# A fused attention, FFN and expert kernel on one Trainium2 core: output clearing, row crossings and GpSimd subtractions put at other places

## The chip, the core and the metric

The kernel runs on one core of one Trainium2 chip. The metric is the device time of one execution in microseconds (us). The engines are named as in the profile: PE (TensorE), ACT (ScalarE), DVE (VectorE), POOL (GpSimd) and SP (SyncE, which here only issues transfers).

## The reference

Three stages follow each other; all data are float32.

```python
# attention: q, k, v are 2 x 8 x 768 x 64; keys seen: the 96 before a row, and the first 8
scores = scale * np.matmul(q, k.transpose(0, 1, 3, 2)) + bias   # ALiBi slopes per head
scores = np.where(is_global | is_local, scores, -1e9)
x = softmax(scores) @ v                     # then 1536 tokens x 512
# gated FFN, d_ff 1536
xn = x / rms * rms_g
x = (silu(xn @ w_gate) * (xn @ w_val)) @ w_out
# router: top 2 of 8 experts, with noise; w1 is 8 x 512 x 1024, w2 is 8 x 1024 x 512
for e in range(E):
    for k in range(2):
        mask = top2[:, k] == e
        h = np.maximum(x[mask] @ w1[e], 0.0)
        out[mask] += top2_w[mask, k, None] * (h @ w2[e])
```

## The kernel before

**Stages.** Attention goes by tiles of 128 rows (L300 to L610): SP loads `kn`, `qn`, `vn` of a tile (L309, L310, L317), PE turns them (L379), makes scores (L427), turns the probabilities (L454) and multiplies with the values (L491). Between these matmuls PE does FFN work of tokens that are ready (`pz` L698). The FFN's weights come in as `rg`, `rv`, `ro` (SP, L630, 512 KB each) and are converted by `conv` (ACT L635, then DVE and POOL); the last of them come while the FFN runs on its own, in the stretch from 200 to 340 us. A routing stage (L793 on) then puts each token's row number and weight into a table in DRAM.

**Two halves of a number.** A product is made of three: each float32 operand is split into an upper part (a copy on ACT) and the rest (a subtraction), and PE multiplies upper with upper, lower with upper and upper with lower. For expert weights `split` (L672) makes `sa` (of w1) and `sb` (of w2): ACT copies (L677), and DVE or POOL subtracts (L681). Which engine subtracts is in one line:

```python
pool = u == 0 and f < 5 if key[0] == "b" else u > 2 and f < 3
```

**Units.** The experts' work goes by `Unit`s n = 0 to 8, each over eight slices f = 0 to 7 of the 1024 hidden columns. Units 2 to 8 have at most 480, 448, 424, 408, 392, 384 and 368 tokens. For each f, `up` multiplies the tokens with a slice of w1 (`pz`, L1034; ACT makes `zh` L1041, DVE `zl` L1042) and `down` multiplies with w2 (`ac`, L1074). The f of unit n run while the tokens of unit n+1 are made ready in `side(f)` of the main loop (L1254 on):

- `gather` (L977): POOL fetches the rows of the tokens from DRAM into `xg`, one indirect transfer per tile of 128 tokens; for units 3 on the rows lie as 16-bit halves.
- `cross` (L982): SP turns a tile by a transposing transfer, `hg<-xg` (L987).
- `turn` (L989): ACT puts the halves together (`xc`, L755) and copies the upper part (`gh`, L996); DVE subtracts (`gl`, L997). `gh` and `gl` are what `up` of unit n+1 reads first.
- `moe2_weights` (L925): SP loads w1's and w2's slice f of unit n+1 (`wab`, L927 and L932, 256 KB each).

**Results.** A unit's result is copied to `oT` as 16-bit halves (ACT L1133, DVE L1131, filled up by a POOL memset L1118), turned by SP transfers `ob<-oT` (L1144) and put together by ACT (`pb`, L1137) at f = 2 and 3 of the next unit; POOL has fetched the tokens' earlier sum (`y<-out_dram`, L1011), DVE adds (L1103), and POOL writes the rows back (`out_dram<-y`, L1107). Rows are added to what is there, so `out` is set to zero once: `clear_out` (L268), one 3 MB transfer on SP's queue, called at L1213.

**What sets the order.** Each engine does its instructions in program order, and a scheduler has put them in that order when the kernel was built; transfers of one issuing engine go out in the order of its program. `follow(a, b)` (L224) makes a stand behind b in the order; it costs no wait by itself. `marks` is the list of the ACT copies of the FFN's hidden blocks (L711), in the order in which they are written down.

Of the kernel before, what the change touches and what calls it, by code (L numbers as in the profile page):

```python
# [10 lines left out]
F32 = mybir.dt.float32  # L11
# [10 lines left out]
P = 128  # L22
# [85 lines left out]
def fused(ctx: ExitStack, tc: tile.TileContext, q, k, v, n_global, n_local, w_gate, w_val, w_out,  # L108
          rms_g, w_router, w_noise, noise, w1, w2, out):
    nc = tc.nc  # L110
# [111 lines left out]
    state = {}  # L222

    def follow(a, b):  # L224
        tc.add_manual_dep(a, b.name, mybir.DependencyInfo(mybir.DependencyClass.NoSync, mybir.DependencyReason.DATA),
                          reason="order")

    def seq(inst):

        if state.get("strict"):  # L230
            if "seq" in state:
                follow(inst.ins, state["seq"])
            state["seq"] = inst.ins
        return inst
# [31 lines left out]
        nc.sync.dma_start(metad.rearrange("(p n) t -> p n t", p=P), dum)  # L266

    def clear_out():  # L268
        nc.sync.dma_start(out.rearrange("(p t) (c d) -> p (t c) d", p=P, d=P),
                            zero.rearrange("p (o d) -> p o d", o=1).broadcast_to([P, NT // P * DC, P]))  # L270

    chosen = keep.tile([P, NT // P, 2, E], F32, name="chosen")
    flag = keep.tile([P, 1], F32, name="flag")
# [398 lines left out]
    def split(key, u):  # L672
        pid = "ab" + key[1:]
        src = raw[pid][:, "ab".index(key[0])]
        f = int(key.split("_")[1])
        wp = pools["b"].tile([P, 2, 512], F32R, name=f"s{key}_{u}", tag="ws", bufs=3)
        cp = nc.scalar.activation(wp[:, 0], src, AF.Copy)  # L677
        if u == 0 and f < 2:
            follow(cp.ins, marks[-4])
        pool = u == 0 and f < 5 if key[0] == "b" else u > 2 and f < 3  # L680
        (nc.gpsimd if pool else nc.vector).tensor_sub(wp[:, 1], src, wp[:, 0].bitcast(F32))  # L681
        return wp[:, 0], wp[:, 1]

    x2t = {}
# [2 lines left out]
    halved = []  # L687
# [248 lines left out]
    class Unit:  # L936
# [45 lines left out]
        def cross(self, s):  # L982
            m = -(-self.tiles[s][1] // 16) * 16
            if s % 2 == 0:
                self.hw = sb.tile([P, 2, 2 * DC, P], U16, name=f"hg{self.n}_{s}", tag="words", bufs=2)
            self.words[s] = self.hw[:, s % 2]
            nc.sync.dma_start_transpose(self.words[s][:, :, :m], self.xg[s][:m])  # L987

        def turn(self, s, behind=None):  # L989
            m = self.tiles[s][1]  # L990
            xg = self.xg.pop(s)
            ss = slice(s * P, s * P + m)
            if self.halved:
                x3 = sb.tile([P, DC, P], F32, name=f"xc{self.n}_{s}", tag="wc", bufs=2)
                merge(x3, self.words[s], m, behind)
                nc.scalar.activation(self.gh[:, :, ss], x3[:, :, :m], AF.Copy)  # L996
                nc.vector.tensor_sub(self.gl[:, :, ss], x3[:, :, :m], self.gh[:, :, ss].bitcast(F32))  # L997
                return
            pt = ps.tile([P, 512], F32, name=f"pg{self.n}_{s}", tag="to"[s % 2])
            p3 = pt.rearrange("p (a b) -> p a b", a=DC)[:, :, :m]  # L1000
            for c in range(DC):
                mm = nc.tensor.transpose(p3[:, c, :], xg[:m, c * P:(c + 1) * P], ident[:m, :m])
                if behind is not None:
                    follow(mm.ins, behind)
            nc.scalar.activation(self.gh[:, :, ss], p3, AF.Copy)
            nc.vector.tensor_sub(self.gl[:, :, ss], p3, self.gh[:, :, ss].bitcast(F32))
# [248 lines left out]
    for i, u in enumerate(units):  # L1255
# [3 lines left out]
        def side(f):  # L1259
            if nxt is not None:  # L1260
                if i == 1:
                    if f == 0:
                        nxt.slots()
                        for s in range(len(nxt.tiles)):
                            nxt.gather(s)
                        for ti in range(G0[LEAD + 1], NT // P):
                            halve(ti, nxt.last.ins)
                elif i and f == (3 if i == 2 else 0):
                    nxt.slots(behind=halved[-1][0] if i == 2 else None)
                    for s in range(len(nxt.tiles)):  # L1270
                        nxt.gather(s)
                if i and f == 6 and i + 2 < len(units):
                    name(units[i + 2])
                    units[i + 2].fetch()
                if i == 1:
                    for s in range(len(nxt.tiles)):
                        if f == 6 + s // 2:
                            nxt.turn(s, u.mark)
                elif i == 0:
                    if f == FB2 - 1:  # L1280
                        for s in range(len(nxt.tiles)):
                            nxt.turn(s, u.mark)
                else:
                    if f in (3, 4):
                        for s in range(len(nxt.tiles))[2 * f - 6:2 * f - 4]:
                            nxt.cross(s)
                    if 8 - len(nxt.tiles) <= f:
                        nxt.turn(f - 8 + len(nxt.tiles), u.act)
            if nw is not None and (i > 1 or f >= AHEAD):
                moe2_weights(nw.wkey, nw.e, f, halved[-1][1] if i == 2 and f == 0 else None)  # L1290
        u.run(side)
    fast.close()

# [86 lines left out]
```

## Time and profile before

| what | value |
|---|---|
| three runs | 769.32, 774.5, 777.71 us; median 774.5 us |
| the profiled execution | 774.73 us |
| its span in the profile | 773.0 us (1.73 us of the execution lie outside) |
| PE busy | 738.5 us, 96% of the span |
| DVE, ACT, POOL busy | 492.3, 408.5, 322.9 us |
| mean granted PE clock | 0.984 of full speed |
| DMA | 107.98 MB, mean 140 GB/s |

A timeline row has the start in us, the duration in us, the engine, the line, the operation with out<-in, and the count of instructions drawn together; in brackets stands how long the engine had been idle before and what ended that. "SPq" is SP's queue of issued transfers: its duration is the time that issuing took, not the time of the transfer. Line numbers are those of the kernel before. The profile comes from one execution, so sums made from it are compared with its own 774.73 us.

### The profile page before, as it was taken

How to read it: one execution, taken by the hardware profiler on the slowest of the kernel's cores; microseconds unless marked ns; L12 is line 12 of the kernel's file. 1: busy time of each engine (PE TensorE's matmuls, PEld its weight loads, DVE VectorE, ACT ScalarE, POOL GpSimd, SP SyncE). 2: the span in 40 equal slices, each digit the busy share in tenths (PEclk: the TensorE clock that was granted, in tenths of full speed). 3: DMA queues.
4: the chain of work that ended last, by engine and by line, in shares of the span. 5: the costliest groups of instructions: out<-in, count | busy, mean ns of one | idle time of the engine just before them, and what ended most of it. 6: DMA issues, size and time to landing. Idle time of an engine off the chain costs nothing.

```text
span 773.0 us, 13551 instructions
## 1 busy us (share of the span) xinstructions
PE 738.5 (96%) x4763; PEld 668.9 (87%) x4763; DVE 492.3 (64%) x1128; ACT 408.5 (53%) x878; POOL 322.9 (42%) x356
## 2 busy tenths in 40 slices
PE   9889989999999999999999999996999999989993
PEld 6679889999988888889999889885999999989993
DVE  7778887887587887334444667733555556666642
ACT  6667657776453443114331465534575767766640
POOL 3237752341476565011633144442254546353511
PEclk9989999999999999999999999998999999999998
DMA  8955365643343330011235413899686979797211
GB/s 195 286 148 141 99 152 93 128 90 73 113 123 106 113 106 0 1 39 71 56 55 116 158 29 104 282 324 204 170 209 165 293 192 328 194 306 171 78 40 37
DMA packets 183160, 107.98 MB, mean 140 GB/s; under 512 B 114193, under 2 KB 165393, under 8 KB 183088
## 3 DMA queue, kind: packets, MB, share of 16 engines
q1 hardware_dynamic: 174240, 84.61, 43.5%
q0 software_dynamic: 7120, 19.32, 8.3%
q10 hardware_dynamic: 1728, 3.15, 1.3%
q8 instruction: 39, 0.64, 0.4%
q14 instruction: 33, 0.27, 0.1%
HBM read 75.23 MB, written 16.49 MB: 119 GB/s over the span
## 4 chain that ended last, share of the span: by engine, by line
PE 78%; DVE 5%; issue 5%; DMA 4%; ACT 3%; SPq 2%; POOL 1%; POOLq 0%; ACTq 0%; DVEq 0%
PE pz L698 16%; PE pz L1034 15%; PE acc L725 12%; PE ac L1074 10%; PE pg L698 5%; PE pv L698 5%; PE ac L1051 4%; PE ps L427 3%; DMA hg<-xg 2%; PE po L495 2%; PE lg L809 1%; PE pt L379 1%; SPq L932 1%; PE po L491 1%; ACT p L434 1%
## 5 line engine op out<-in xcount | busy, mean ns | idle before, releaser
L1034 PE MATMUL pz<-gh,sa 128*128 128x256 f32 (+7 forms) x576 | 153.4, 335 | 0.0
L1034 PEld LDWEIGHTS pz<-gh,sa 128*128 128x128 f32 x576 | 103.8, 188 | 4.6
L1034 PE MATMUL pz<-gl,sa 128*128 128x256 f32 (+7 forms) x288 | 96.3, 336 | 2.0 <-DVE gl L997 2.0
L1074 PE MATMUL ac<-zh,sb 128*128 128x480 f32 (+4 forms) x320 | 86.5, 363 | 6.1 <-ACT sb L677 6.1
L725 PE MATMUL acc<-wo,dh 128*128 128x512 f32 x288 | 88.1, 398 | 0.5 <-ACT dh L711 0.5
L698 PE MATMUL pz<-xTh,wg 128*128 128x256 f32 x352 | 75.6, 291 | 0.5 <-DVE u L708 0.5
L698 PE MATMUL pz<-xTh,wv 128*128 128x256 f32 x352 | 74.7, 290 | 0.0
L1041 ACT ACTIVATE zh<-pz 128x256 fp32r<-128x256 f32 (+7 forms) x72 | 35.1, 487 | 73.9 <-PE pz L1034 73.9
L1042 DVE SCALAR_TENSOR_TENSOR zl<-pz,zh 128x256 fp32r<-128x256 f32 (+7 forms) x72 | 39.7, 551 | 51.6 <-ACT zh L1041 51.3
L681 DVE TENSOR_TENSOR sb<-wab,sb 128x512 fp32r<-128x512 f32 x67 | 48.8, 729 | 32.7 <-ACT sb L677 30.9
L1074 PEld LDWEIGHTS ac<-zh,sb 128*128 128x128 f32 x320 | 60.6, 191 | 9.9 <-ACT sb L677 6.6
L698 PEld LDWEIGHTS pz<-xTh,wg 128*128 128x128 f32 x352 | 60.2, 196 | 2.8 <-DVE u L708 0.8
L1107 POOL DMA_INDIRECT out_dram<-y,me x30 | 33.8, 1128 | 64.5 <-DVE y L1103 57.8
L677 ACT ACTIVATE sa<-wab 128x512 fp32r<-128x512 f32 x72 | 44.9, 625 | 29.6 <-PE ac L1074 15.6
L698 PEld LDWEIGHTS pz<-xTh,wv 128*128 128x128 f32 x352 | 59.1, 194 | 0.8
L725 PEld LDWEIGHTS acc<-wo,dh 128*128 128x128 f32 x288 | 51.1, 189 | 8.9 <-ACT dh L711 0.7
L1034 PEld LDWEIGHTS pz<-gl,sa 128*128 128x128 f32 x288 | 54.0, 188 | 5.1 <-DVE gl L997 2.6
L712 POOL TENSOR_TENSOR dl<-u,dh 128x256 fp32r<-128x256 f32 (+1 forms) x38 | 37.6, 990 | 44.5 <-ACT dh L711 24.6
L1074 PE MATMUL ac<-zl,sb 128*128 128x480 f32 (+4 forms) x160 | 53.1, 362 | 0.0
L698 PE MATMUL pz<-xTl,wg 128*128 128x256 f32 x176 | 51.3, 291 | 1.9 <-DVE xTl L600 1.9
L725 PE MATMUL acc<-wo,dl 128*128 128x512 f32 x144 | 52.9, 396 | 0.0
L1051 PE MATMUL ac<-sb,zh 128*128 128x512 f32 (+1 forms) x176 | 50.9, 376 | 0.3 <-DVE sb L681 0.3
(255 smaller groups left out, 1839.6 us busy)
## 6 DMA issues: line engine op xcount, KB each, us to landing
wab<-in_moe_w_dram SPq DMA_DIRECT2D x128, 256.0 KB, 5.4
rg<-in_moe_w_gate_dram SPq DMA_DIRECT2D x12, 512.0 KB, 4.9
rv<-in_moe_w_val_dram SPq DMA_DIRECT2D x12, 512.0 KB, 3.7
ro<-in_moe_w_out_dram SPq DMA_DIRECT2D x12, 512.0 KB, 3.4
vn<-in_v_dram SPq DMA_DIRECT2D x12, 256.0 KB, 4.0
out_dram<-zero SPq DMA_DIRECT2D x1, 3072.0 KB
x2d<-x ACTq DMA_DIRECT2D x12, 256.0 KB, 5.8
x2p<-hw SPq DMA_DIRECT2D x12, 256.0 KB, 5.0
```

The lines of the kernel that those rows point to most:

```text
L427: seq(nc.tensor.matmul(o, qT[a, h], kT[c][sl, h // 2, C0:], start=(n == 0), stop=(n == len(prods) - 1)))
L677: cp = nc.scalar.activation(wp[:, 0], src, AF.Copy)
L681: (nc.gpsimd if pool else nc.vector).tensor_sub(wp[:, 1], src, wp[:, 0].bitcast(F32))
L698: mm = nc.tensor.matmul(pz, a[:, cs], x[:, tt:tt + nt, c, :], start=(n == 0), stop=(n == 3 * DC - 1))
L712: (nc.gpsimd if ci < len(CHUNKS) - 1 else nc.vector).tensor_sub(dl, u, dh.bitcast(F32))
L725: nc.tensor.matmul(acc[t], a[:, tt], w, start=(f == CHUNKS[ci][0] and n == 0), stop=(end and n == 2))
L1034: mm = nc.tensor.matmul(pz[:, :cap], a[:, cs], x[:, c, :cap], start=(k == 0), stop=(k == 3 * DC - 1))
L1041: self.act = nc.scalar.activation(dh[:, :cap], pz[:, :cap], AF.Relu).ins
L1042: nc.vector.scalar_tensor_tensor(dl[:, :cap], pz[:, :cap], 0.0, dh[:, :cap].bitcast(F32), op0=ALU.max, op1=ALU.subtract)
L1051: mm = nc.tensor.matmul(o, a[:, s * P:s * P + m], w[:, cuts(s)[x]], start=(f == 0 and k == 0), stop=(f == FB2 - 1 and k == 2)).ins
L1074: nc.tensor.matmul(acc[c][:, :cap], w[:, c * P:(c + 1) * P], a[:, :cap], start=(f == 0 and k == 0), stop=(f == FB2 - 1 and k == 2))
L1107: st = nc.gpsimd.indirect_dma_start(out=out, out_offset=bass.IndirectOffsetOnAxis(ap=self.me[:m, s, 0:1], axis=0), in_=y[:m], in_offset=No ...
```

## The change

Three edits. First, the transfer that clears `out` must stand behind the last entry of `marks` at that point of the program. Second, the four (or three) crossings of the next unit's tiles are asked for together, at f = 3 of unit 2 and at f = 2 of later units, in place of two at f = 3 and two at f = 4; and from that f on, the next unit's weight loads must stand behind the last crossing in the order. Third, POOL subtracts for `sa` at f = 1 and 2 alone (f = 0 goes to DVE) in units 3 on, and each such subtraction waits, by a semaphore (`hold`), for the last `gl` that DVE was given.

```diff
+    def hold(a, b):
+        tc.add_manual_dep(a, b.name, mybir.DependencyInfo(mybir.DependencyClass.Sync, mybir.DependencyReason.DATA),
+                          reason="order")
...
     def clear_out():
-        nc.sync.dma_start(out.rearrange("(p t) (c d) -> p (t c) d", p=P, d=P),
+        cl = nc.sync.dma_start(out.rearrange("(p t) (c d) -> p (t c) d", p=P, d=P),
                             zero.rearrange("p (o d) -> p o d", o=1).broadcast_to([P, NT // P * DC, P]))
+        follow(cl.ins, marks[-1])
...
-        pool = u == 0 and f < 5 if key[0] == "b" else u > 2 and f < 3
-        (nc.gpsimd if pool else nc.vector).tensor_sub(wp[:, 1], src, wp[:, 0].bitcast(F32))
+        pool = u == 0 and f < 5 if key[0] == "b" else u > 2 and 0 < f < 3
+        sub = (nc.gpsimd if pool else nc.vector).tensor_sub(wp[:, 1], src, wp[:, 0].bitcast(F32))
+        if pool and u:
+            hold(sub.ins, state["gl"])
...
-            nc.sync.dma_start_transpose(self.words[s][:, :, :m], self.xg[s][:m])
+            self.crossed = nc.sync.dma_start_transpose(self.words[s][:, :, :m], self.xg[s][:m]).ins
...
-                nc.vector.tensor_sub(self.gl[:, :, ss], x3[:, :, :m], self.gh[:, :, ss].bitcast(F32))
+                state["gl"] = nc.vector.tensor_sub(self.gl[:, :, ss], x3[:, :, :m], self.gh[:, :, ss].bitcast(F32)).ins
...
-                    if f in (3, 4):
-                        for s in range(len(nxt.tiles))[2 * f - 6:2 * f - 4]:
+                    if f == (3 if i == 2 else 2):
+                        for s in range(len(nxt.tiles)):
                             nxt.cross(s)
...
-                moe2_weights(nw.wkey, nw.e, f, halved[-1][1] if i == 2 and f == 0 else None)
+                moe2_weights(nw.wkey, nw.e, f, halved[-1][1] if i == 2 and f == 0 else nw.crossed if i > 1 and f >= (3 if i == 2 else 2) else None)
```

SP's queue in the attention stage, before: `metad`, `wr` and `nz` are small tables, `out_dram<-zero` is the clearing, and the next rows load the attention's fourth tile and FFN weights.

```order
L217 DMA nz<-in_moe_noise_dram 128x12x8
L269 DMA out_dram<-zero 6144x1x128
L309 DMA kn_397<-in_k_dram 128x8x64
L310 DMA qn_396<-in_q_dram 128x8x64
L317 DMA vn_421<-in_v_dram 128x8x64
L630 DMA ro_594<-in_moe_w_out_dram 128x1024
```

The same place of SP's queue after, and then the place at which the clearing stands now, among the last FFN weights.

```order
L217 DMA nz<-in_moe_noise_dram 128x12x8
L314 DMA kn_397<-in_k_dram 128x8x64
L315 DMA qn_396<-in_q_dram 128x8x64
L322 DMA vn_421<-in_v_dram 128x8x64
L635 DMA ro_594<-in_moe_w_out_dram 128x1024
...
L635 DMA ro_3750<-in_moe_w_out_dram 128x1024
L273 DMA out_dram<-zero 6144x1x128
L635 DMA rg_3811<-in_moe_w_gate_dram 128x4x256
L635 DMA rv_3872<-in_moe_w_val_dram 128x4x256
```

The loads of `kn_397` and of all after it lose one 3 MB transfer ahead of them; `rg_3811` and what comes after it get it.

SP's queue while unit 2 runs, before: `wab_6` and `wab_7` are unit 3's last weights, the next `wab_0` and `wab_1` are already unit 4's, and `hg` are the crossings of unit 3's four tiles.

```order
L932 DMA wab_6_6573<-in_moe_w_dram 128x512
L927 DMA wab_7_6617<-in_moe_w_dram 128x4x128
L987 DMA_TRANSPOSE hg_0_6426<-xg_0_6418 128x8x128
L932 DMA wab_7_6617<-in_moe_w_dram 128x512
L927 DMA wab_0_6709<-in_moe_w_dram 128x4x128
L987 DMA_TRANSPOSE hg_0_6426<-xg_1_6420 128x8x128
L932 DMA wab_0_6709<-in_moe_w_dram 128x512
...
L932 DMA wab_1_6732<-in_moe_w_dram 128x512
L987 DMA_TRANSPOSE hg_2_6467<-xg_2_6422 128x8x128
L987 DMA_TRANSPOSE hg_2_6467<-xg_3_6424 128x8x64
```

The same crossings after:

```order
L934 DMA wab_2_6376<-in_moe_w_dram 128x4x128
L939 DMA wab_2_6376<-in_moe_w_dram 128x512
L994 DMA_TRANSPOSE hg_0_6426<-xg_0_6418 128x8x128
L994 DMA_TRANSPOSE hg_0_6426<-xg_1_6420 128x8x128
L994 DMA_TRANSPOSE hg_2_6429<-xg_2_6422 128x8x128
L994 DMA_TRANSPOSE hg_2_6429<-xg_3_6424 128x8x64
L934 DMA wab_3_6432<-in_moe_w_dram 128x4x128
```

All four crossings have moved to behind unit 3's `wab_2`: the first ahead of nine weight loads that it stood behind, the last two ahead of fourteen.

POOL's order in a later unit, before: the subtractions of unit 4's `sa`, then the stores of unit 3's results, the gathers for unit 6, and the loads of earlier sums `y`, up to the next unit's subtractions.

```order
L681 TENSOR_TENSOR sa_0_4_7083<-wab_0_6709,sa_0_4_7083 128x512
L681 TENSOR_TENSOR sa_1_4_7118<-wab_1_6732,sa_1_4_7118 128x512
L1118 MEMSET oT_1_7465 128x8x88
L681 TENSOR_TENSOR sa_2_4_7156<-wab_2_6770,sa_2_4_7156 128x512
L1107 DMA out_dram<-y_0_6883,me_6198 1536x512
...
L962 TENSOR_SCALAR ic_7509<-me_7379 128x4
L977 DMA xg_0_7513<-x2p,ic_7509 128x1024
...
L977 DMA xg_3_7519<-x2p,ic_7509 16x1024
L1011 DMA y_0_7289<-out_dram,ic_6697 128x512
...
L681 TENSOR_TENSOR sa_0_5_7489<-wab_0_7115,sa_0_5_7489 128x512
```

POOL's order after, from the stores of unit 3's results on:

```order
L1114 DMA out_dram<-y_0_6883,me_6198 1536x512
...
L1114 DMA out_dram<-y_3_7026,me_6198 1536x512
L1018 DMA y_0_7289<-out_dram,ic_6697 128x512
...
L1018 DMA y_3_7432<-out_dram,ic_6697 40x512
L969 TENSOR_SCALAR ic_7509<-me_7379 128x4
L984 DMA xg_0_7513<-x2p,ic_7509 128x1024
...
L984 DMA xg_3_7519<-x2p,ic_7509 16x1024
L686 TENSOR_TENSOR sa_1_5_7524<-wab_1_7138,sa_1_5_7524 128x512
L686 TENSOR_TENSOR sa_2_5_7562<-wab_2_7182,sa_2_5_7562 128x512
```

The gathers stood among the stores and ahead of the loads of `y`; they now stand behind these, last ahead of the two subtractions, and `sa_0` is gone from POOL.

## Rows read from the trace of the kernel before

**Rows 1.** The page's first part: busy us, share, instructions of each engine
```profile
PE 738.5 (96%) x4763; PEld 668.9 (87%) x4763; DVE 492.3 (64%) x1128; ACT 408.5 (53%) x878; POOL 322.9 (42%) x356
```
**Rows 2.** SP's queue, 514 to 523 us, crossings among weight loads
```profile
514.77 2.07 SPq L987 DMA_TRANSPOSE hg<-xg  x1
...
521.43 2.94 SPq L987 DMA_TRANSPOSE hg<-xg  x1
```
**Rows 3.** ACT's timeline, unit 2's last f
```profile
537.13 1.34 ACT L755 ACTIVATE xc<-hg 128x1024 uint16<-128x1024 uint16 x1 [8.91 <-DMA hg<-xg]
```
**Rows 4.** PE's timeline, from unit 2's last up to unit 3's first
```profile
530.05 0.38 PE L1034 MATMUL pz<-gh,sa 128*128 128x480 f32 x1
...
532.47 0.38 PE L1034 MATMUL pz<-gh,sa 128*128 128x480 f32 x1
539.00 2.37 PE L1074 MATMUL ac<-zh,sb 128*128 128x480 f32 x5 [6.15 <-ACT sb L677]
...
546.43 0.36 PE L1034 MATMUL pz<-gh,sa 128*128 128x448 f32 x1
```
**Rows 5.** Windows: length, busy PE PEld DVE ACT POOL, PE clock, DMA share, GB/s
```profile
200.00:340.00 140.00, 140.00 (x674) 116.82 (x673) 99.14 (x132) 51.44 (x89) 68.12 (x62) 1.00 0.23 71
...
540.00:545.00 5.00, 5.00 (x17) 4.20 (x16) 2.74 (x4) 2.52 (x5) 1.70 (x2) 0.63 1.01 309
```
**Rows 6.** POOL's timeline, last gather for unit 3
```profile
507.00 0.92 POOL L977 DMA_INDIRECT xg<-x2p,ic  x1 [0.30 <-PE pz L1034]
```
**Rows 7.** DMA view, 495 to 545 us: gathers, count, median us to landing
```profile
xg<-x2p,ic POOLq DMA_INDIRECT x8, 7.0
```
**Rows 8.** All crossings `hg` of the kernel
```profile
DMA to landing us min/median/max: 3.8/5.5/13.9
```
**Rows 9.** DVE's timeline, end of unit 6
```profile
686.71 0.75 DVE L997 TENSOR_TENSOR gl<-xc,gh 128x512 fp32r<-128x512 f32 x1
...
690.88 3.67 DVE L997 TENSOR_TENSOR gl<-xc,gh 128x512 fp32r<-128x512 f32 x1 [1.69 <-ACT gh L996]
```
**Rows 10.** POOL's timeline, end of unit 6
```profile
691.47 2.52 POOL L681 TENSOR_TENSOR sa<-wab,sa 128x512 fp32r<-128x512 f32 x2
```
**Rows 11.** PE's timeline, start of unit 7
```profile
694.60 0.61 PE L1034 MATMUL pz<-gl,sa 128*128 128x384 f32 x2 [1.95 <-DVE gl L997]
```
**Rows 12.** SP's queue in the attention stage
```profile
17.99 0.69 SPq L269 DMA_DIRECT2D out_dram<-zero  x1
19.09 9.36 SPq L309 DMA_DIRECT2D kn<-in_k_dram  x1
```
**Rows 13.** PE's timeline in the attention stage, waits over 1.5 us
```profile
32.49 0.63 PE L379 MATMUL pt<-ident,kn 128*128 128x128 f32 x4 [1.95 <-DMA kn<-in_k_dram]
...
40.23 0.66 PE L454 MATMUL pp<-ident,p 128*128 128x128 f32 x4 [1.93 <-ACT pf L457]
...
43.85 0.58 PE L698 MATMUL pz<-xTl,wg 128*128 128x256 f32 x1 [1.88 <-DVE xTl L600]
```
**Rows 14.** A window of the attention stage, columns as in rows 5
```profile
44.00:46.00 2.00, 2.00 (x10) 2.00 (x11) 1.16 (x6) 1.65 (x5) 1.22 (x1) 0.50 0.71 253
```
**Rows 15.** SP's queue and then ACT, around 260 us: rg_3811 loaded and used
```profile
260.57 0.37 SPq L630 DMA_DIRECT2D rg<-in_moe_w_gate_dram  x1
...
277.10 0.66 ACT L635 ACTIVATE wcg<-rg 128x512 f32<-128x512 f32 x1
```
**Rows 16.** POOL's timeline in unit 4, and the next unit's first matmul
```profile
609.74 0.95 POOL L1107 DMA_INDIRECT out_dram<-y,me  x1 [0.30 <-issue]
...
615.59 0.98 POOL L1011 DMA_INDIRECT y<-out_dram,ic  x1 [0.59 <-DMA out_dram<-y,me]
...
620.35 2.55 POOL L681 TENSOR_TENSOR sa<-wab,sa 128x512 fp32r<-128x512 f32 x2
...
622.43 0.34 PE L1034 MATMUL pz<-gh,sa 128*128 128x408 f32 x1
```
**Rows 17.** ACT's timeline in unit 4: the last results of unit 3 put together
```profile
600.01 2.58 ACT L1137 ACTIVATE pb<-ob 128x1024 uint16<-128x1024 uint16 x2
```

## The prediction

> **What bounds the kernel now.** I read the page's shares first: PE is busy for 738.5 of 773.0 us [rows 1], so all that any change can give without taking matmuls away lies in the 34.5 us in which PE stands, and in stretches in which PE runs at the lower clock. The change takes no matmul away. I then went through PE's timeline for waits and read for each what ended it; three places belong to the three edits.
>
> Place A is the seam of units 2 and 3. PE's last matmul ahead of it starts at 532.47, the next at 539.00, after 6.15 us of waiting for ACT's copy of `sb` [rows 4]. ACT was late because it had stood 8.91 us for a crossing [rows 3]; that tile's crossing had been issued at 521.43 [rows 2], 15.7 us ahead of the copy. SP issued the first crossing at 514.77 and the third at 521.43 [rows 2], although the gathers had been issued by 507.9 [rows 6]: they stood behind weight loads. After the wait PE pays again: the 24 matmuls of that `down` take from 539.00 to 546.43, which is 0.31 us each, where eleven of the same width took 0.22 each ahead of the wait (530.05 to 532.47) [rows 4]; the granted clock there is 0.63 [rows 5].
>
> Place B is the seam of units 6 and 7: PE waits 1.95 us for `gl` [rows 11]. This `gl` took DVE 3.67 us where the one before it took 0.75 [rows 9], and beside it POOL did two subtractions, from 691.47 to 693.99 [rows 10].
>
> Place C is the attention stage around 32 to 48 us. PE waits 1.95, 1.93 and 1.88 us [rows 13], the first time for `kn`. SP had issued the clearing of `out` at 17.99, and the issue of `kn` right behind it lasted 9.36 us [rows 12]. Behind the last wait PE runs at the lower level, half speed (1.2 in place of 2.4 GHz) [rows 14].
>
> **Part 1: the crossings of unit 3.** They now stand behind `wab_2` in SP's program. The load right ahead of them is issued at about 504, the last gather at 507.0 with a median landing of 7.0 us [rows 6, 7], so SP waits until about 514 and the last crossing goes out at about 517 (four of some 2 us each [rows 2], partly while the later gathers are still on their way); with the median landing of 5.5 us [rows 8] it is there at about 522, while ACT wanted the third tile at 537.13 - 8.91 = 528.2 [rows 3] and the fourth one slice later. So all of the 6.15 us goes, and with the wait the slow clock after it: 24 times (0.31 - 0.22) = 2.1 us. Term A: -8.3 us. What is late next: SP has nothing else to issue while it waits for the gathers, so unit 3's `wab_3` and later ones go out from about 517 in place of 504 on. They are needed from the fourth slice of unit 3, some 14 us after its start (546.43, or 538 when A is gone), that is 30 us later.
>
> **Part 2: the crossings of later units.** Units 3 to 7 show no wait of PE for a crossing or a weight load, so the gain is nothing. Their weights from `wab_2` on now go out behind four crossings, so later by what these hold the queue (two to three us each, and the wait until ACT has emptied the buffers that the results' crossings `ob` used, 602.59 in unit 4 [rows 17], 17 us into the unit). The first of them, `wab_2`, is then issued some 20 us into a unit of 36 us and wanted by ACT one to two slices of 4.5 us into the next, so more than 15 us later; a load has 5.5 us at the page's median of crossings [rows 8] or 13.9 at worst. I take 0, bounds 0 and +5 (one microsecond in each of five units, if the cover is gone).
>
> **Part 3: POOL's subtractions.** Where POOL's pair ran beside it, `gl` grew from 0.75 to 3.67 us [rows 9, 10]; the `hold` forbids that, so `gl` ends at about 691.6, ahead of the 692.14 at which the unit's first matmul began. Term B: -1.95 us [rows 11], once; at the other seams PE did not wait for `gl`. Six more subtractions of `sa_0` fall to DVE, 0.7 us each going by `gl` of the same width [rows 9]; DVE stands idle before `gl` for longer (1.69 us in brackets [rows 9]), so I take them at 0; bound: 6 x 0.7 = 4.2 us if that idle time were gone. The Trainium skill ("SBUF — State Buffer", section "SBUF: two separate sides") says that a VectorE instruction with two SBUF inputs and a GpSimd one that reads SBUF share an exclusive port pair, and that whichever starts first has it for its whole instruction. Here `gl` starts at 690.88, ahead of POOL's 691.47, and still ends 0.56 us behind POOL [rows 9, 10], so the row has the later one win. By the page's rule `gl` would have been late for another reason, term B would be 0 and the sum 761.0; I go by the row.
>
> **Part 4: the clearing.** Without it `kn` goes out at about 18 to 19 us and is issued in well under a microsecond; its 9.36 us of issue time [rows 12] go, and the rest of the fourth tile and the FFN weights behind it on SP come some 9 us earlier. At most that gives the three waits, 5.76 us, and half of the 4.9 us from 43.85 to about 48.7 that PE worked at half clock [rows 13, 14], 2.4 us: 8.2 us. At least it gives nothing, if the tile's later chain through ACT and DVE is as late without it: only the first of the three waits names `kn`, the others name ACT's `pf` and DVE's `xTl` [rows 13]. The scheduler has also drawn attention forward and pushed some FFN matmuls back in this stage. I take 5.5 us, nearer to the top, since the later two waits are those of the tile that `kn` starts. Term C: -5.5 us. In its new place the 3 MB pass in a stretch with a DMA share of 0.23 and PE without a gap (140.00 of 140.00) [rows 5]. The cover is the lead of the weights: `rg` behind it is issued at 260.57 and first used at 277.10 [rows 15], 16.5 us. The clearing held the queue for about 10.5 us (17.99 to 28.45) [rows 12], and a landing takes 5.5 us at the median of the crossings [rows 8], so about half a microsecond is left on this reckoning; behind it lies a second cover, that a weight which ACT has converted is used by PE later still. If both were gone each missing microsecond would cost one. I take 0, bound +4.
>
> **The sum.** 774.73 - 8.3 - 1.95 - 5.5 = 759.0 us. The profiled execution and the median of the runs shown (774.5) differ by 0.2 us, so this stands against both: 2.0% less. About 1% (7.7 us) is what a measurement of this kernel can tell from no change.
>
> **The rivals.** (1) *Attention gives nothing.* For it: two of three waits in C name ACT and DVE. Against it: the order in which the three follow each other. Then 774.73 - 10.25 = 764.5, still faster by over 1%. (2) *The crossing is late anyway.* The one that PE waited for took 13.9 us from issue to landing where the median is 5.5 [rows 8]; if gathers and crossing are slow because all transfers are (a GB/s of over 300 at that time, as in the last row of [rows 5]), the crossings go out at 521 again and only some 2 us of A go; with half of C (2.75) and B: 774.73 - 2 - 1.95 - 2.75 = 768.0, within 1%. Against it: in the new order fourteen 256 KB loads are not ahead of the crossings but behind. (3) *Slower, POOL's chain comes late.* The gathers now stand behind the loads of `y`, which wait for the stores, and the next unit's `sa_1` stands last. In the profiled unit 4 the last store went out at 609.74, the first `y` load at 615.59, 5.85 later, and the subtraction pair began at 620.35, 2.08 ahead of the next unit's first matmul [rows 16]. Three gathers were issued in those 5.85 us for nothing; now all four come after the loads, about 1.2 us each (0.92 and 0.30 [rows 6]). On the other side the stores no longer wait for gathers: ACT had put the last results together by 602.59 [rows 17], so the last store goes out at about 604. By the same steps (5.85 + 4 x 1.2 + 4 x 1.2 + 0.5) `sa_1` begins at about 620 and ends at 621.3; it is wanted about 2 us into the next unit, at 624.5. So some 3 us are left, 1 to 2 in the shorter later units. If each link from store to load to gather took 13.9 us [rows 8] in place of 5.85, the chain would be 8 us later or more, and five seams would pay about 5 us each: 759.0 + 25 = 784. It decides against the change from 15.7 / 5 = 3.1 us of payment a seam on, that is some 5 us later than I reckon. A smaller slip (1 us a seam) gives 764. By the page's rule on the port pair, B gives nothing: 761.0, with a chance of 0.1 as the rows bear it out, inside the forecast's own neighbours. (4) *The whole of C, and a little more from seams that I count as free*: 756.
>
> **How the numbers follow.** Chances: forecast with its near neighbours (756 to 762) 0.55; attention gives nothing or POOL slips a little (762 to 767) 0.26; the crossing is late anyway or several slips add up (767 to 782) 0.13; slower through POOL's chain 0.06. The range of 8 in 10 is 752 to 769: below, the whole of C and another 4 us at seams that run at the lower clock; above, rival 2. Faster by over 1% (under 766.8): 0.81; within 1%: 0.13; slower: 0.06.
>
> **What would show it.** Right: SP issues four crossings before 518 with the next weight load behind them; ACT's `xc` of unit 3 has no wait of several microseconds and PE none between 520 and 545; `gl` at every seam lasts about 0.75 us and PE's wait ahead of unit 7 is gone; `kn` of the fourth tile is issued at about 19 us in under 1 us, and PE between 30 and 50 us is busy for some 5 us more, at the full clock; no wait of PE between 255 and 290. Wrong: waits of PE for POOL's `sa` about 2 us into units 4 to 8, each with a late `y` load or gather ahead of it on POOL; waits for a `wab` from the third slice on; new waits in attention that name ACT or DVE and add up to what C lost; a gap at about 275 us behind `rg`.

## The result and the profile after

The changed kernel took 763.06 us in the median of four runs (762.17 to 764.36), the kernel before 771.91 us beside it (768.9 to 777.71). The ratio is 0.9892, 95% interval 0.9852 to 0.9932: 8.3 us less of 771.9, clear of no change. A later set of twelve runs gave 0.9913 (0.9885 to 0.9941). Slow executions, of 1034 to 4125 us (one each of e9 and e11, two of the kernel before), are left out of every ratio and median here. The forecast was 759.0 us with a range of 752 to 769: the direction and the range hold, but the time lies in the class of 762 to 767 us, which had a chance of 0.26, and the gain is 8.9 us by the medians in place of the sum's 15.75.

The profiled execution of the changed kernel took 762.32 us (span 760.5); that of the kernel before took 774.73, 2.8 us more than its own median. So 12.4 us lie between the two profiles and 8.9 between the medians, and these 3.5 us are about half of the 6.9 by which the forecast's gain was too large. First the page's line of shares, which answers to [rows 1]:

```profile
PE 735.9 (97%) x4763; PEld 666.6 (88%) x4763; DVE 485.8 (64%) x1134; ACT 410.2 (54%) x878; POOL 318.8 (42%) x350
```

PE does the same 4763 matmuls; its busy time is 2.6 us shorter, with less of it at the lower clock (the mean granted clock is 0.994 in place of 0.984), and 9.9 us of standing are gone (34.5 before, 24.6 now).

**Place A, the seam of units 2 and 3.** The changed kernel's SP queue, which answers to [rows 2], and a window of it (length, then busy time of PE, PEld, DVE, ACT, POOL, PE clock, DMA share, GB/s):

```profile
505.29 6.28 SPq L994 DMA_TRANSPOSE hg<-xg  x4
511.82 0.43 SPq L934 DMA_DIRECT2D wab<-in_moe_w_dram  x1
```
```profile
530.00:545.00 15.00, 15.00 (x75) 13.67 (x74) 7.33 (x14) 8.16 (x19) 2.59 (x2) 1.00 0.32 73
```

The four crossings go out together by 511.6, the next weight load behind them; PE is busy throughout, at the full clock. Part 1 happened as it was written, with the crossings out some 5 us ahead of the 517 that it reckoned.

**Place B, the seams.** DVE's last `gl` ahead of unit 7, which answers to [rows 9]:

```profile
680.02 0.69 DVE L686 TENSOR_TENSOR sa<-wab,sa 128x512 fp32r<-128x512 f32 x1 [1.16 <-ACT sa L682]
680.63 0.69 DVE L1004 TENSOR_TENSOR gl<-xc,gh 128x512 fp32r<-128x512 f32 x1
```

`sa` of f = 0 is DVE's now, and PE waits for none of DVE's in units 3 to 8; `gl` takes 0.69 us in place of 3.67, and so does every full `gl` of units 3 to 8. PE's wait ahead of unit 7 is gone.

**Place C, attention.** SP's queue, which answers to [rows 12], and PE's waits of over 0.8 us up to 200 us that answer to [rows 13] or are new:

```profile
16.73 0.51 SPq L217 DMA_DIRECT2D nz<-in_moe_noise_dram  x1
22.34 0.37 SPq L314 DMA_DIRECT2D kn<-in_k_dram  x1
```
```profile
30.99 0.63 PE L459 MATMUL pp<-ident,p 128*128 128x128 f32 x4 [1.00 <-DVE pf L464]
...
42.20 0.39 PE L705 MATMUL pz<-xTh,wg 128*128 128x256 f32 x1 [1.29 <-ACT wg L653]
...
150.48 0.66 PE L599 MATMUL px<-ident,x 128*128 128x128 f32 x4 [1.10 <-DVE x L586]
...
158.59 0.20 PE L500 MATMUL po<-vn,ph 128*128 128x64 bf16 x1 [0.88 <-DMA ph<-h]
```

`kn` is issued in 0.37 us in place of 9.36, at 22.34 and not at 18 to 19 as reckoned; the three waits of 5.76 us have become two of 2.29, and the stretch at half clock is gone. But 150 us in stand two new waits, of attention's own chain; from 50 to 200 us PE stands 5.4 us in place of 4.4. The FFN's last block before the experts, the same `acc<-wo,dh` matmul in both, starts at 438.69 where it started at 442.19, so 3.5 us are ahead there.

These 3.5 us are less than attention gave, because the two profiled executions had unequal starts. Two of PE's rows, the kernel before first, then the changed one; PE's program is the same up to there:

```profile
8.09 0.71 PE L427 MATMUL ps<-kT,qT 64*128 64x128 f32 x4
10.27 0.56 PE L491 MATMUL po<-vn,pf 128*128 128x64 f32 x4
```
```profile
10.05 1.22 PE L432 MATMUL ps<-kT,qT 64*128 64x128 f32 x4
14.05 0.56 PE L496 MATMUL po<-vn,pf 128*128 128x64 f32 x4
```

The same four `ps` take 1.22 us in place of 0.71, and the first `po` starts 3.8 us later. The clock column has 1.00 for this stretch in both profiles, so only the durations show it. In the fourteen profiled executions a single `idle` matmul drops from 0.6 to 0.4 us somewhere between 4.4 and 16.4 us: at 4.4 in the kernel before, at 15.2 in the changed kernel and at 10.7 in e10, which is the same program. So 7.3 us were won between 10 and 440 us. In e7, which has the same attention and a start as quick as the first profile's, `kn` is issued at 18.75 and the FFN block starts at 436.28, 5.9 us ahead of 442.19.

In its new place the clearing does no harm:

```profile
251.56 0.67 SPq L273 DMA_DIRECT2D out_dram<-zero  x1
257.07 6.22 SPq L635 DMA_DIRECT2D rg<-in_moe_w_gate_dram  x1
```

The load behind it is held for 6.22 us, and PE has no wait between 200 and 340 us.

**A new wait.** POOL in unit 4, which answers to [rows 16], the table's load on SP, and PE's first wait in unit 5:

```profile
600.47 1.11 POOL L1018 DMA_INDIRECT y<-out_dram,ic  x1 [0.30 <-issue]
608.03 0.47 POOL L969 TENSOR_SCALAR ic<-me 128x4 int32<-128x4 int32 x1 [6.45 <-DMA me<-metad]
...
612.65 0.86 POOL L984 DMA_INDIRECT xg<-x2p,ic  x1 [0.30 <-issue]
613.54 2.50 POOL L686 TENSOR_TENSOR sa<-wab,sa 128x512 fp32r<-128x512 f32 x2
```
```profile
599.03 0.50 SPq L957 DMA_DIRECT2D me<-metad  x1
```
```profile
614.87 0.64 PE L1041 MATMUL pz<-gh,sa 128*128 128x408 f32 x2 [1.28 <-POOL sa L686]
```

POOL's gathers stand behind the table `me` (their list of rows). SP issues it at 599.03, behind the crossings and eight weight loads, 25 us after unit 4's first matmul (573.90); in the kernel before it went out ahead of the crossings, 11 us after that matmul (596.88 against 585.63). POOL waits 6.45 us for it, so `sa` begins at 613.54, and PE waits 1.28 us for `sa`. The five tables of 4 KB also take longer to land (the last column is the median in us of those landings that the profile has; the kernel before first, then the changed one):

```profile
me<-metad SPq DMA_DIRECT2D x5, 4.0 KB, 4.2
```
```profile
me<-metad SPq DMA_DIRECT2D x5, 4.0 KB, 7.0
```

This is the third rival in its small form.

### The profile page after: what moved, and what is told of

It is laid out like the page before. It is cut to its first block, busy times and chain, and to the rows that moved or that the text cites. A ratio compares the mean times of both kernels' runs of the same rounds, so it can differ in the third digit from the quotient of the medians.

```text
span 760.5 us, 13550 instructions
## 1 busy us (share of the span) xinstructions
PE 735.9 (97%) x4763; PEld 666.6 (88%) x4763; DVE 485.8 (64%) x1134; ACT 410.2 (54%) x878; POOL 318.8 (42%) x350
## 4 chain that ended last, share of the span: by engine, by line
PE 79%; DVE 7%; DMA 5%; issue 4%; ACT 2%; POOL 1%; SPq 0%; POOLq 0%; ACTq 0%; DVEq 0%
PE pz L1041 17%; PE pz L705 14%; PE acc L732 12%; PE ac L1081 11%; PE pg L705 5%; PE pv L705 5%; PE ac L1058 5%; PE ps L432 3%; PE po L500 1%; DMA ph<-h 1%; PE lg L816 1%; DMA rv<-in_moe_w_val_dram 1%; PE pt L384 1%; PE po L496 1%; DMA y<-out_dram,ic 1%
## 5 line engine op out<-in xcount | busy, mean ns | idle before, releaser
L1081 PE MATMUL ac<-zh,sb 128*128 128x480 f32 (+4 forms) x320 | 84.7, 357 | 0.0
L705 PE MATMUL pz<-xTh,wg 128*128 128x256 f32 x352 | 73.9, 286 | 1.3 <-ACT wg L653 1.3
L705 PEld LDWEIGHTS pz<-xTh,wg 128*128 128x128 f32 x352 | 58.3, 190 | 3.8 <-ACT wg L653 1.5
L686 DVE TENSOR_TENSOR sa<-wab,sa 128x512 fp32r<-128x512 f32 x60 | 44.6, 745 | 23.6 <-ACT sa L682 23.1
```

Of the source, the lines that this page charges most:

```text
L686: sub = (nc.gpsimd if pool else nc.vector).tensor_sub(wp[:, 1], src, wp[:, 0].bitcast(F32))
L705: mm = nc.tensor.matmul(pz, a[:, cs], x[:, tt:tt + nt, c, :], start=(n == 0), stop=(n == 3 * DC - 1))
L1081: nc.tensor.matmul(acc[c][:, :cap], w[:, c * P:(c + 1) * P], a[:, :cap], start=(f == 0 and k == 0), stop=(f == FB2 - 1 and k == 2))
```

## The experiments

Each was timed against the kernel before on the same chip; the median of before lay between 770.1 and 773.2 us in the four sets, so the ratios are what can be compared.

| label | edit | ratio, 95% interval |
|---|---|---|
| e1 | before + clearing moved | 0.9927 (0.9900 to 0.9955) |
| e2 | before + crossings | 1.0050 (1.0027 to 1.0073) |
| e3 | before + subtractions | 0.9965 (0.9939 to 0.9990) |
| e4 | after, clearing back | 0.9920 (0.9889 to 0.9952) |
| e5 | after, `me` fetched early | 0.9931 (0.9904 to 0.9958) |
| e6 | after, POOL at f = 2 alone | 0.9894 (0.9857 to 0.9931) |
| e7 | after, no `hold` | 0.9902 (0.9868 to 0.9936) |
| e8 | after, weights not behind crossings | 0.9946 (0.9915 to 0.9977) |
| e9 | after, no crossing edit | 0.9925 (0.9884 to 0.9966) |
| e10 | after again | 0.9913 (0.9885 to 0.9941) |
| e11 | after, POOL at f = 2 alone, no `hold` | 0.9845 (0.9814 to 0.9876) |

**One part alone: e1, e2, e3, and one undone: e4.** e1 is the kernel before with the clearing's new place alone (the transfer also gets the name `cl`):

```diff
+        follow(cl.ins, marks[-1])
```

> The kernel before with the clearing alone put behind the FFN's marks. Theory (the clearing's gain is partly given back by attention itself): PE's waits for kn, pf and xTl and the half clock between 32 and 49 us are gone, PE is some 7 us ahead at 100 us, but new waits of PE for attention's own chain (DVE, transfers of h) between 100 and 160 us take back about half, so 3.5 us are left at the first expert matmul and the time is about 768.4 us. Rival (the give-back comes from the other two edits, which change the scheduler's order): 7 us stay, about 765 us. Rival 2 (nothing in attention was the clearing's doing): 772 us.

5.6 us less in time, between the theory and its rival. The profile has the theory's picture: the waits at 150 us are in the clearing's own trace, so the other edits did not bring them.

```profile
150.52 0.66 PE L595 MATMUL px<-ident,x 128*128 128x128 f32 x4 [1.40 <-DVE x L582]
158.80 0.20 PE L496 MATMUL po<-vn,ph 128*128 128x64 bf16 x1 [1.04 <-DMA ph<-h]
439.17 1.20 PE L726 MATMUL acc<-wo,dh 128*128 128x512 f32 x4 [0.47 <-ACT dh L712]
531.28 1.34 PE L1075 MATMUL ac<-zh,sb 128*128 128x480 f32 x5 [1.11 <-ACT sb L678]
```

At 439.17 PE is 3.0 us ahead of the first profile. The last row was not expected: the seam of units 2 and 3 waits 1.11 us in place of 6.15, with the crossings untouched. And the wait ahead of unit 7 is gone, with the subtractions untouched: that `gl` ended 0.79 us ahead of POOL's pair.

```profile
682.77 0.69 DVE L998 TENSOR_TENSOR gl<-xc,gh 128x512 fp32r<-128x512 f32 x1 [1.69 <-ACT gh L997]
684.25 2.54 POOL L682 TENSOR_TENSOR sa<-wab,sa 128x512 fp32r<-128x512 f32 x2
```

e2 is the kernel before with the crossing edit alone, the weights behind `nw.crossed` with it:

```diff
-                    if f in (3, 4):
-                        for s in range(len(nxt.tiles))[2 * f - 6:2 * f - 4]:
+                    if f == (3 if i == 2 else 2):
+                        for s in range(len(nxt.tiles)):
```

> The kernel before with the crossings and the order of the weights alone. Theory: the stall at the seam of units 2 and 3 goes whole (8.5 us in the profiled executions), and POOL's chain costs about 1 us at a seam of units 4 to 6: 764 to 765 us, PE without a wait between 520 and 545 us. Rival (the profiled execution of before had a long stall, others a shorter one): the profile's gain is 8.5 but the median's only some 5, 767 us.

Both were wrong: alone, the crossing edit makes the kernel 3.9 us slower. The stall at the seam of units 2 and 3 is gone, and in its place stand four waits for POOL's `sa`, one in each of units 4 to 7:

```profile
580.51 0.65 PE L1034 MATMUL pz<-gh,sa 128*128 128x424 f32 x2 [2.73 <-POOL sa L681]
...
622.16 1.05 PE L1034 MATMUL pz<-gh,sa 128*128 128x408 f32 x2 [2.99 <-POOL sa L681]
...
661.47 0.63 PE L1034 MATMUL pz<-gh,sa 128*128 128x392 f32 x2 [2.15 <-POOL sa L681]
...
696.87 0.63 PE L1034 MATMUL pz<-gh,sa 128*128 128x384 f32 x2 [0.74 <-POOL sa L681]
```
```profile
573.70 0.24 POOL L962 TENSOR_SCALAR ic<-me 128x4 int32<-128x4 int32 x1 [5.53 <-DMA me<-metad]
574.38 1.07 POOL L977 DMA_INDIRECT xg<-x2p,ic  x1 [0.44 <-POOL ic L962]
...
578.28 0.88 POOL L977 DMA_INDIRECT xg<-x2p,ic  x1 [0.30 <-issue]
579.17 2.52 POOL L681 TENSOR_TENSOR sa<-wab,sa 128x512 fp32r<-128x512 f32 x2
```
```profile
575.00:585.00 10.00, 7.27 (x29) 6.54 (x28) 5.78 (x8) 4.13 (x10) 6.38 (x7) 0.83 0.96 258
```

POOL waits 5.53 us for `me`, then does four gathers and only then `sa` of f = 0 and 1. The window shows what that costs: in 10 us PE is busy for 7.27, and the mean granted clock is 0.83, so part of it passed at half speed. The waits sum to 8.6 us, and the clock comes on top.

e3 is the kernel before with the subtractions alone, the `hold` with them:

```diff
-        pool = u == 0 and f < 5 if key[0] == "b" else u > 2 and f < 3
+        pool = u == 0 and f < 5 if key[0] == "b" else u > 2 and 0 < f < 3
```

> The kernel before with POOL's subtractions alone (f = 0 to DVE, the rest held behind gl). Theory (gl is slow because POOL's subtraction runs beside it): every gl at a seam under 0.8 us, PE's wait of 1.95 us at unit 7 gone, 770 us; the stall for the crossing stays. Rival (by the page's rule the first to start keeps the port, and gl was late for another reason): a gl of over 1.3 us at some seam stays, 772 us.

2.7 us less. Every full `gl` takes 0.68 or 0.69 us and the wait of 1.95 us is gone, as the theory has it; but e1 and e2 have that too, so this profile alone does not show that the edit did it. In this execution too PE waited only 0.58 us at the seam of units 2 and 3, against what was expected, although ACT stood 8.1 us for crossings there (3.01, 2.35 and 2.78, at three tiles). By e2 and e4 the same edit is worth far more beside the crossings: from 1.0050 (crossings) to 0.9920 (crossings and subtractions) are 10 us, because POOL then has `sa` of f = 0, the most urgent one, no longer behind its gathers: e2's four waits of 8.6 us are one of 0.90 in e4.

e4 is the changed kernel with the clearing back (the name `cl` goes too):

```diff
-        follow(cl.ins, marks[-1])
```

> The changed kernel with the clearing back at its old place. Theory: the changed kernel's 763.1 us and 3.5 us on top, 766.6 us, with the waits for kn, pf and xTl back at 32 to 44 us. Rival (seven microseconds hang on it, and the order of the other edits gives them back): 770 us.

The theory's number, 766.3 us. The waits for `kn`, `pf` and `xTl` are back at 32.06, 39.96 and 43.59, with 1.54, 2.10 and 1.85 us.

**Is the stall always there? e0, the kernel before once more.**

> The kernel before once more, for its profile. Theory (the length of the stall at the seam of units 2 and 3 changes from execution to execution, with the landing of the third crossing): the wait of PE there differs by 2 us or more from the 6.15 us of the first profile, and by about as much this execution's time differs from 774.7 us, while the waits in attention (1.95, 1.93, 1.88 us) and the 1.95 us ahead of unit 7 come again within 0.3 us. Rival (the stall is the same in each execution, and something else scatters): 5.9 to 6.4 us again.

The theory holds for the stall, and more sharply than written: PE did not wait at that seam at all. ACT's third `xc` of unit 3 stood for 1.22 us, where [rows 3] has 8.91:

```profile
532.11 1.38 ACT L755 ACTIVATE xc<-hg 128x1024 uint16<-128x1024 uint16 x1 [1.22 <-DMA hg<-xg]
```
```profile
544.91 0.68 PE L1034 MATMUL pz<-gh,sa 128*128 128x448 f32 x2 [1.37 <-POOL sa L681]
...
615.05 1.22 PE L1074 MATMUL ac<-zh,sb 128*128 128x424 f32 x5 [1.31 <-ACT sb L677]
...
691.89 0.62 PE L1034 MATMUL pz<-gl,sa 128*128 128x384 f32 x2 [1.89 <-DVE gl L997]
```

But the time did not follow: 772.01 us is 2.7 less than 774.73, not 8. PE reached unit 2 2.7 us later than in the first profile (498.51 against 495.84), reached unit 3 5.9 us earlier (540.56 against 546.43), and then lost 3.4 of these by unit 6 (655.44 against 657.87), with two waits that the first did not have (1.37 and 1.31 us; the 1.89 for `gl` came again). The waits in attention came again as 1.82, 1.34 and 1.88 us; the second is 0.6 off, outside what was expected. The program is the same to the instruction; at that seam what differs is how long ACT stood for the same transfer.

**What the crossing edit is worth in company: e8 and e9, with e10 beside them.**

e8 is the changed kernel with the weights not ordered behind the crossings:

```diff
-                moe2_weights(nw.wkey, nw.e, f, halved[-1][1] if i == 2 and f == 0 else nw.crossed if i > 1 and f >= (3 if i == 2 else 2) else None)
+                moe2_weights(nw.wkey, nw.e, f, halved[-1][1] if i == 2 and f == 0 else None)
```

> The changed kernel with the weight loads no longer ordered behind the crossings (the crossings are still asked for together and at the earlier f). The scheduler then puts unit 3's crossings back behind wab_7, as in the kernel before. Theory: it is the order of the weights that moves the crossings; ACT stands again for xc of unit 3, by 1 to 9 us as the landing falls, and the ratio to the kernel before is 0.990 to 0.996 with a wider scatter than the changed kernel's. Rival: asking earlier is what gives, 0.988 to 0.990, no wait of ACT over 1 us.

Ratio and scatter are the theory's (761.9 to 770.8 us, five of twelve runs over 768), but in the profiled execution ACT did not stand for `xc` of unit 3 at all, as little as the rival asked. So the order of the weights is what moves the crossings, and in this execution it would not have mattered.

e9 is the changed kernel with the whole crossing edit undone, that of e8 with it:

```diff
-                    if f == (3 if i == 2 else 2):
-                        for s in range(len(nxt.tiles)):
+                    if f in (3, 4):
+                        for s in range(len(nxt.tiles))[2 * f - 6:2 * f - 4]:
```

> The changed kernel without the crossing edit: clearing and subtractions alone. Theory A (the three gains are independent and the crossing is worth its 8.3 us): ratio about 0.999, 771 us, a wait of PE of some 6 us at the seam of units 2 and 3. Theory B (the stall is long in few executions, and clearing alone, 0.9927, and subtractions alone, 0.9965, already make up the change's 0.989): ratio 0.988 to 0.991, with a wider scatter than the changed kernel's and a wait for xc between 0 and 9 us.

Nearest to theory B, a little over its 0.988 to 0.991: 0.9925 with clearing and subtractions alone, against 0.9892 and 0.9913 with the crossings too; the intervals overlap. The runs fall in two heaps, five from 762.2 to 765.3 and two at 771.9 and 772.1 us. ACT's wait for `xc` in the profiled one, a run of the upper heap, is 1.41 us and PE's none, so what made that run long was not the crossing either: it was 5.8 us behind the changed kernel's profile at the last FFN block (444.46 against 438.69) and 8.7 at unit 2's first matmul (501.39 against 492.66), before any crossing of unit 3.

e10 is the changed kernel itself.

> The changed kernel once more, beside these two on one chip. Theory: ratio 0.987 to 0.991; no wait of PE at the seam of units 2 and 3 and none for gl; one or two waits for POOL's sa of 0.5 to 2 us about 4 us into units 4 to 7, not always at the same unit. Rival (the wait of 1.28 us at unit 5 is fixed by the order): 1.1 to 1.5 us at unit 5 again and none elsewhere.

Theory: two waits for `sa`, 0.60 and 0.80 us, in units 4 and 5, where the first profile had one of 1.28 in unit 5. Eleven of its twelve runs lie from 763.3 to 766.9, the last at 769.4.

**POOL's chain and the wait: e5, e6, e7, e11.** e5 asks for `me` four slices earlier:

```diff
-                if i and f == 6 and i + 2 < len(units):
+                if i and f == (2 if i > 2 else 6) and i + 2 < len(units):
```

> The changed kernel with the next but one unit's table me fetched at f = 2, ahead of the crossings, in place of f = 6 behind eight weight loads (SP, units 3 on). Theory (in the changed kernel POOL's chain is late because the gathers wait for me): ic no longer waits several us for me, the gathers go out before the y loads, POOL's sa is in time at every seam and the wait of 1.28 us in the middle of units 4 and 5 goes: 761.8 us (1.3 less than 763.1). Rival (the chain is late because y loads and gathers are too many): a wait of about 1 us for POOL's sa stays, 763 us.

Neither. In units 4 and 5 the wait for `sa` is gone, as the theory had it, but the scheduler answered with another order on POOL, and in unit 6 a gather and its wait for `me` now stand between `sa` of f = 1 and of f = 2; PE waits 2.07 us there, and the kernel is slower than the changed one by the middle of the ratios, though the intervals overlap.

```profile
649.70 1.31 POOL L686 TENSOR_TENSOR sa<-wab,sa 128x512 fp32r<-128x512 f32 x1
654.48 0.55 POOL L969 TENSOR_SCALAR ic<-me 128x3 int32<-128x3 int32 x1 [3.47 <-DMA me<-metad]
655.31 1.05 POOL L984 DMA_INDIRECT xg<-x2p,ic  x1 [0.28 <-PE ac L1081]
656.39 1.27 POOL L686 TENSOR_TENSOR sa<-wab,sa 128x512 fp32r<-128x512 f32 x1
```

e6 leaves POOL one subtraction a unit:

```diff
-        pool = u == 0 and f < 5 if key[0] == "b" else u > 2 and 0 < f < 3
+        pool = u == 0 and f < 5 if key[0] == "b" else u > 2 and f == 2
```

> The changed kernel with POOL subtracting at f = 2 alone, so that sa of f = 1 goes to DVE too. Theory: what POOL's late chain has to deliver is wanted 4.5 us later, no PE wait for POOL's sa stays: 761.8 us. Rival (DVE's 0.69 us more ahead of a seam makes zl or the oT copies late): DVE waits appear on PE at the seams, 764 us or more.

No wait of PE for POOL's `sa` is left, and none for DVE at the seams; the ratio, 0.9894, is the changed kernel's within what these runs tell apart, so the gain of 1.3 us is neither shown nor excluded.

e7 takes the semaphore wait away:

```diff
-        if pool and u:
-            hold(sub.ins, state["gl"])
```

> The changed kernel without the semaphore wait (hold), the rest as it is; POOL's order is the same. Theory A (the order alone keeps POOL's subtractions clear of gl, since they now stand behind loads and gathers): all gl but unit 8's last stay under 0.8 us, 763.1 us within 0.7. Theory B (the hold is what gives): gl of over 1.3 us at two or more seams, 765 us.

Theory A: no `gl` of units 3 to 8 takes over 0.8 us without the semaphore, and 0.9902 is the changed kernel's ratio. The wait itself does nothing that can be measured here. What keeps POOL clear of `gl` is the order: that `sa` of f = 0 is gone from it, or that gathers stand ahead of its subtractions. Which of the two is not told apart; in e2, with f = 0 still on POOL and no `hold`, every full `gl` took 0.68 or 0.69 us too.

e11 is e6 and e7 together.

> The changed kernel with POOL subtracting at f = 2 alone and without the semaphore wait. Theory (what helps is that POOL has less to do near a seam, the wait is not needed): ratio 0.988 to 0.992 as the changed kernel's, no wait of PE for POOL's sa, every gl but at most one under 0.8 us. Rival (the wait protects gl): a gl of over 1.3 us at two or more seams and a ratio over 0.992.

0.9845, under the 0.988 to 0.992 of its theory, and the fastest kernel of the study: 759.1 us (five runs) where the kernel before took 770.1. From 490 us to the end PE has no wait of over 0.25 us in its profile. It differs from e6 in the `hold` alone; their intervals overlap (0.9857 to 0.9931 against 0.9814 to 0.9876), so whether the wait costs something beside two fewer subtractions on POOL stays open. Its interval lies below that of e10 and overlaps that of the first set.

## Why the prediction was right, and where it was wrong

Between the two profiles the account closes. The changed kernel's was 3.5 us ahead at the last FFN block, 3.2 at unit 2's first matmul, 11.7 at unit 3's (546.43 against 534.71), 10.1 at unit 6's (657.87 against 647.77) and 12.5 at unit 8's (727.69 against 715.15). So the stall of A gave 8.5 us and the `gl` of B 2.4, both as forecast or more; C gave 2.0 less than its 5.5, and the new wait for `sa`, counted at 0, took most of the 1.6 lost from unit 3 to unit 6. The rest of the miss, 3.5 us, is that the two profiled executions lie further apart than the medians.

**Term A (-8.3 us): mechanism right, size wrong.** The step that failed is the one that took 6.15 us of waiting and 2.1 us of slow clock from [rows 3] and [rows 4] as what the kernel before loses there. That is what one execution lost. Six profiled executions have unit 3's crossings in the old order (the first, e0, e1, e3, e8, e9), and PE waited 6.15, 0, 1.11, 0.58, 0 and 0 us at that seam. The forecast's worst landing of 13.9 us [rows 8] comes from the same four crossings: the profile gives it to the fourth, issued at 524.46, and has no landing of the third, for which PE waited. It was used as a bound for others and not seen as the reason why A itself was long. And when the stall was short, other waits took part of its place (e0). What the crossing edit adds to the other two, 0.9925 to 0.9892 or 0.9913, is 1 to 2.5 us by the middle values and not told apart from nothing.

**Term B (-1.95 us): right by the times, as one execution's value again.** e3 alone gives 2.7 us (0.8 to 4.7), and the wait is in neither of the changed kernel's profiles. Both executions of the kernel before have it (1.95 and 1.89 us), but e1 and e2 do not, with the subtractions untouched: there POOL's pair began after `gl` had ended. That a `gl` grows beside POOL's `sa` is seen at other seams too (the last, narrow one took 3.16 us in the first profile, 3.07 in e0 and 3.12 in e1), where PE waited for none. The reason given, the `hold`, was wrong: e7 has the same `gl` without it. The sum of 761.0, by the rule of the Trainium skill, is nearer to the measured 763.1, but not for its reason: the wait that it keeps is gone. On the rule itself (the Trainium skill, "SBUF — State Buffer", section "SBUF: two separate sides") the trace differs in one point: in e0, as in [rows 9, 10], `gl` started 0.53 us ahead of POOL's pair (688.22 against 688.75) and ended 0.57 us behind it (691.84 against 691.27). That both cannot work at once agrees.

**Term C (-5.5 us): mechanism right, size about right where starts are equal.** PE's row at 440 us gives 3.0 us (e1) to 3.5 (the changed kernel) against the first profile, but both had long first matmuls; where these were short in both profiles it gives 5.9 (e7 against the first), and where they were long in both 7.4 (e1 at 439.17 against e3 at 446.56). That e1 alone takes 5.6 us off the time (3.5 to 7.7) is in part luck: its profile has the stall of A at 1.11 us and no wait for `gl`, which the clearing does not explain. By e4 and the first set it is 2 us, with overlapping intervals. The waits named in part 4 went nearly whole; the part that the forecast had only in general words, that attention's chain through DVE and the transfers is late for itself, came 100 us later: 1.98 us of new waits at 150 to 159 us, 1.0 us more in all from 50 to 200. The new place of the clearing cost nothing, as reckoned.

**Rival 3, POOL's chain: the mechanism is real.** The forecast gave it 0.06 for a slower kernel and counted 3 us of slack; it left out the table `me`, which stands behind weight loads on SP that were themselves put behind the crossings (6.45 us of waiting on POOL). The place where it decides was underrated: with `sa` of f = 0 still on POOL (e2) it costs four waits of 0.74 to 2.99 us and makes the kernel slower. The change as a whole escapes it because its third part takes away the subtraction that is needed first. The forecast priced that move as a cost to be hidden (0, at most +4.2 us); beside the crossings it was worth 10 us (e2 against e4).

**What stays open.** The medians of the parts (5.6, -3.9, 2.7) do not add up to the whole; that crossings and subtractions depend on each other is shown, how much of the rest is scatter is not. Why the crossing's landing takes longer in some executions, and why the first matmuls stay slow for 4 to 16 us, was not tried. Nor is it settled whether the clearing's place has a part in the latter: the drop came after 6 us in one of the five executions with the old place and in eight of the nine with the new one.

## What to carry to other kernels

A stall whose length is that of one transfer's landing can be a draw, as it was here, and then it is not a term: before it goes into a sum, look at the scatter of the runs (here 8.4 us between the three that were shown, as much as the term) and take a second profile. Before two profiles are compared stage by stage, compare a short row near their start. When transfers are put ahead of others on an in-order queue, follow the smallest of those put back (here a 4 KB table) to whoever waits for it, and from there to what is queued behind that wait on the other engine. What an engine must deliver first should not stand behind its waits for transfers: moving that one short operation to another engine made the difference between a slower kernel (e2) and a faster one (e4).

## What was not expected of the hardware

A short wait of PE can cost more than its length, and need not: in e2 the window around the wait of 2.73 us has a mean granted clock of 0.83, the one around the wait of 2.15 us (656 to 666 us) has 1.00. The same program, to the instruction, waited 6.15 us at one place in one execution and not at all in another, with a difference of 2.7 us in all. And the same program ran its first matmuls slowly until 15.2 us in one execution and until 10.7 in another, with 1.00 in the clock column of both.
